# The first transform unit of a mixing one stretch later, and a mixing that ends with its last unit

## The chip, the cores and the metric

The kernel runs on one core of one Trainium2 chip. The metric is the device time of one execution in microseconds (us), as the median of several runs. A profile of one further execution shows every instruction of every engine: TensorE (PE) does the matrix products and the transposes, VectorE (DVE), ScalarE (ACT) and GpSimd (POOL) the elementwise work, SyncE (SP) issues most of the transfers.

## The reference

Two blocks in a row, all in fp32, for 8 batches, 8 heads, 576 positions and 64 values per head:

```python
scores = matmul(q, k.T) / sqrt(64)                    # (8, 8, 576, 576)
thresh = max(scores, -1) - tau
scores = where(scores >= thresh, scores, -1e9)
attn = exp(scores - max(scores)); attn /= sum(attn) + 1e-9
x = matmul(attn, v)                                   # rearranged to (8, 576, 512)

mixed = real(fft(fft(x, axis=1), axis=2))             # over positions, then over values
u = x + mixed
un = (u - mean(u)) / sqrt(var(u) + 1e-6)
out = u + maximum(un @ w_ch1, 0) @ w_ch2              # w_ch1 512x2048, w_ch2 2048x512
```

## The kernel before

The attention is cut into steps: a step is 128 queries (64 for the last) of a pair of heads, five steps make a pair of heads, four pairs a batch, so 20 steps make a batch (`per_batch`) and the eight batches 160 steps. A step computes the scores (`sc`, lines 440 and 446), takes their maximum (`neg`, VectorE, line 520), the exponentials (ScalarE, line 526), the threshold and the sum (VectorE, line 540), the division (ScalarE, line 549), and transposes the weights on TensorE (`pe`, line 587, and `pw`, line 605), which ScalarE copies out of PSUM. Twice in five steps the product with the values (`pv`, line 636) is made.

The two Fourier transforms of a batch are matrix products with cosine and sine tables. When the last pair of heads of a batch is done, its rows are folded (sums and differences of mirrored positions, lines 687 to 703, on VectorE for the last pair), and a generator `mixing` (line 728) does the rest in units, each ended by a `yield`. Its first three units are folds on VectorE into the tile `f` (lines 718 to 749). Six units follow in which TensorE multiplies `f` with the tables over the values (`py`, line 759) and ScalarE copies the result to `y_e` or `y_o` (line 764). The last five multiply with the tables over the positions (`pa`, lines 776 and 780), and VectorE and GpSimd add `x` and store to `u_t` (lines 796 to 805).

The channel products of the reference are done for groups of 512 rows, by a product of two levels with fewer multiplications, in the generator `two_level`: 28 items of first-level products (`ph`, line 1203) and 49 items of second-level products (`po`, line 1390). An item of `po` is four to eight matmuls and counts 2048 columns; seven items share two PSUM banks (four and three), which VectorE, ScalarE or GpSimd drain or add up (lines 1184, 1402 to 1410, 1255, 1336). A group can only begin when the mixing of its batch is at its end (`mixed`).

The order of everything is written out by hand[...]. From batch 2 on (line 1724) a step is a row of three stretches, and each has one call of `fill`. `fill` adds `per_slot` columns to a budget and works off items of the groups until what is spent reaches the budget. `per_slot` is set when a batch's mixing is started (`start_batch`, line 1622, in the step whose number in its batch is 2): what is to do, less `keep`, over 60 stretches. `keep` is thus the work that is left over when the next mixing starts. A unit of a mixing counts against the budget with what it yields, MIX / 11 for each matrix unit and nothing for the folds.

Units are taken by `mix(1)`. In step 2 of a batch the mixing begins: one unit after the first `fill`, one in the second. In step 3 the third fold is taken before the first `fill`, and so is one unit between the first and the second `fill`, one in the second and one in the third. From step 4 on there is one unit in each stretch. These are the lines in the loop:

```python
        fill(True)
        ...softmax_second(i), measure(), what was held...
        if mixes:
            mix(1)
        ...
        weights = weights_in_parts(i - 1) if i <= total else iter(())
        next(weights, None)          # pe and the first pw
        ...
        fill()
        next(weights, None)          # the second pw
```

`fill(True)` takes no unit of a mixing; `fill()` takes one before its items. PSUM tiles named pd, pm, pn, pe, pw, pv, py, pa, ph and po come from one ring of four banks with the tag "mm".

After the last step the remaining items and the last mixing follow in a tail, and then groups 7 and 8 alone.

Of the kernel before, what the change touches and what calls it, by code (L numbers as in the profile page):

```python
# [18 lines left out]
def _reversed(ap):  # L19

    n = ap.shape[1]
    return bass.AP(
        tensor=ap.tensor,
        offset=ap.offset + n - 1,
        ap=[list(ap.ap[0]), [-1, n]],
    )
# [21 lines left out]
def kernel(  # L48
# [14 lines left out]
    DM = H * D  # L63
# [5 lines left out]
    NJ = HID // 128  # L69
# [7 lines left out]
    BT = 512  # L77
# [645 lines left out]
    MIX = 4 * (3 * 5 * 128 + 5 * 2 * KH)  # L723
# [4 lines left out]
    def mixing(b):  # L728
# [43 lines left out]
        def over_seq(y, odd, cols, m):  # L772
            pa = ps.tile([128, 512], FP32, tag="mm", bufs=4, name="pa")
            for parity, u, table, extra in ((0, 0, seq_even, seq_xe), (1, 2, seq_odd, seq_xo)):
                at = pa[0:m, parity:KH:2]
                nc.tensor.matmul(  # L776
                    at, y[:, u, cols], table[:, odd, :], start=True, stop=False,
                    skip_group_check=True,
                )
                nc.tensor.matmul(  # L780
                    at, y[:, 1, cols], extra[:, odd, :], start=False, stop=True,
                    skip_group_check=True,
                )
            return pa

        settle(b)
        for t in range(2):
            cols = slice(128 * t, 128 * t + 128)
            tmp = sb.tile([128, 3, KH], FP32, tag="tmp", bufs=1, name="tmp")
            low, high, sin = (tmp[:, c, :] for c in range(3))  # L790
            pb = over_seq(y_o, 1, cols, 128)
            nc.scalar.copy(sin, pb[:, 0:KH])
            yield MIX / 11
            pa = over_seq(y_e, 0, cols, 128)

            nc.vector.tensor_tensor(out=low, in0=pa[:, 0:KH], in1=sin, op=ALU.subtract)  # L796
            nc.vector.tensor_tensor(out=high, in0=pa[:, 0:KH], in1=sin, op=ALU.add)
            def add(c, rows, first, second, eng=None):
                if eng is None:
                    eng = nc.vector if b == B - 1 and c % 2 else nc.gpsimd  # L800
                eng.tensor_tensor(  # L801
                    out=u_t[rows, c, slot.start : slot.start + KH],
                    in0=x[c][rows, 0:KH], in1=first, op=ALU.add,
                )
                eng.tensor_tensor(
                    out=u_t[rows, c, slot.start + KH : slot.stop],
                    in0=x[c][rows, KH:S], in1=_reversed(second[:, 1:HALF]), op=ALU.add,
                )

            every = slice(0, 128)  # L810
            add(t, every, low, high, nc.vector if b == 0 and t == 1 else nc.gpsimd)
            add(3 - t, every, high, low)
            if t == 1:
                add(3, slice(0, 1), high[0:1, :], low[0:1, :])
            yield MIX / 11
            if t == 1:

                pa = over_seq(y_e, 0, slice(256, 257), 1)
                nc.scalar.copy(sin[0:1, :], pa[0:1, 0:KH])
                add(2, slice(0, 1), sin[0:1, :], sin[0:1, :])  # L820
                yield MIX / 11


    warm = const.tile([128, 1], FP32, name="warm")
# [2 lines left out]
    def measure():  # L827
        while measures:
            measures.pop(0)()
# [5 lines left out]
    def cost(g):  # L835

        return (4 * BT * (NJ * ND + NJ * DM // 128) if g == 0 else COLS1 + COLS2) + ND * BT
# [59 lines left out]
    def channels(rows):  # L897
        for j in range(NJ):
            ht = hs[:, BT * j : BT * (j + 1)]
            ph = ps.tile([128, 512], FP32, tag="mm", bufs=4, name="ph")  # L900
            for c in range(ND):
                nc.tensor.matmul(  # L902
                    ph[:, :], w1[c][:, 128 * j : 128 * (j + 1)], u_t[:, c, 0:BT],
                    start=(c == 0), stop=(c == ND - 1),
                )
            if j % 2 == 0:
                nc.scalar.activation(out=ht, in_=ph[:, :], func=ACT.Relu)
            else:
                nc.vector.tensor_relu(ht, ph[:, :])
            yield 4 * ND * BT  # L910
            if j % 3 == 2 and j // 3 < 4:
                rows.load(j // 3)
                yield ND * 128
            if j == 12:
                rows.factors()
        def both():
            yield from w1_forms()
            ensure(1)
            while not next(forms_w2):
                yield  # L920

        forms = both()
        for t in range(4):
            po = ps.tile([128, DM], FP32, tag="mm", bufs=4, name="po")
            for j in range(NJ):
                nc.tensor.matmul(  # L926
                    po[:, :], hs[:, BT * j + 128 * t : BT * j + 128 * (t + 1)], w2[j],
                    start=(j == 0), stop=(j == NJ - 1),
                )
                if j % 2 == 1 and j < NJ - 1:  # L930
                    next(forms, None)
                    yield 2 * 4 * DM
            rows.add(t, slice(0, DM), po[:, :])
            rows.store(t)
            background()
            yield 2 * 4 * DM
        for _ in forms:
            pass
# [531 lines left out]
    mixes = []  # L1470
    mixed = 0
    work = []
    spent = budget = per_slot = 0.0
    per_batch = NPAIR * NT
# [143 lines left out]
    def fold_more():  # L1618
        if folds and next(folds[0], True):
            folds.pop(0)  # L1620

    def start_batch(b):

        nonlocal groups, todo, per_slot, budget
        mixes.append(mixing(b))
        todo += MIX
        while groups < NG and BT * (groups + 1) <= (b + 1) * S:
            rows = Rows(groups)
            work.append((b, channels(rows) if groups == 0 else two_level(groups, rows), rows))
            todo += cost(groups)  # L1630
            groups += 1

        keep = 4 * BT * NJ * DM // 128 if b == 0 else 3 * 7 * 2048
        per_slot = (todo - spent - keep) / (3 * per_batch)
        budget = spent

    def mix(count):
        nonlocal spent, mixed
        for _ in range(count):
            done = next(mixes[0], None)  # L1640
            if done is None:
                mixes.pop(0)
                mixed += 1
                break
            spent += done

# [77 lines left out]
    for i in range(2 * per_batch, total):  # L1724


        n, t = divmod(i, NT)
        values = iter(())
        if i < total:
            scores(i)  # L1730
        if t == 3 and i < total:
            values = values_in_parts(n, 0)
        elif t == 1 and n > 0:
            while folds:
                fold_more()
            values = values_in_parts(n - 1, 1)
        next(values, None)
        if i % per_batch == 3:
            next(values, None)
        if i < total:  # L1740
            softmax_first(i)
        next(values, None)
        if i % per_batch == 3:
            mix(1)
        if i % per_batch == 2:
            for _ in last_fold:
                pass
            start_batch(i // per_batch - 1)
        fill(True)
        if i < total:  # L1750
            softmax_second(i)
        measure()
        while held:
            held.pop(0)()
        if mixes:
            mix(1)
        if t == 1:
            if n % NPAIR:
                folds.append(fold_rows(n - 1))
            else:  # L1760
                last_fold = fold_rows(n - 1)
                next(last_fold)
        weights = weights_in_parts(i - 1) if i <= total else iter(())
        next(weights, None)
        if t > 2:
            fold_more()
        fill()
        if i % per_batch == 1:
            next(last_fold)
        next(weights, None)  # L1770
        if i < total:
            softmax_third(i)
            if t == 1:
                prep_ends(n)
            if t == 2 and n + 1 < B * NPAIR:
                scale_q(n + 1)
            if t == 3 and n + 1 < B * NPAIR:
                prep_pair(n + 1)
        if wanted:
            wanted.pop().factors()  # L1780
        if i % per_batch == 1:
            next(last_fold)
        fill(apart=i % per_batch == 2)
        if t == 2 and n + 1 < B * NPAIR:
            load_v(n + 1)
        if t == 4 and n + 2 < B * NPAIR:
            load_pair(n + 2)
# [89 lines left out]
```

## Time and profile before

| | |
|---|---|
| median of 3 runs | 1574.24 us (1571.42 to 1574.62) |
| the profiled execution | 1571.58 us, its span 1569.8 us, mean granted TensorE clock 0.996 |
| TensorE busy with matmuls | 1526.0 us |
| VectorE, ScalarE, GpSimd busy | 1061.6, 916.4, 777.5 us |
| DMA | 239.31 MB, 152 GB/s on average |

In the lines of the profile, L759 is line 759 of the kernel, `py<-dim_c,f` says that `py` is written from `dim_c` and `f`, and x4 that four instructions are merged. In the timeline the first number is the start in us from the span's start, the second the duration; what stands in brackets is the idle time of the engine ahead of the instruction and what ended it. In the waits the numbers are the sum in us, how often, and the longest.

### The profile page before, as it was taken

The page shows a single profiled execution, that of the slowest core. Times are in us where ns is not written, and L with a number is a line of the kernel's source. Part 1 is how long each engine was busy: PE and PEld are TensorE (multiplying, and loading weights), DVE is VectorE, ACT ScalarE, POOL GpSimd, SP SyncE. Part 2 cuts the span into 40 slices and gives each one's busy share as a digit, 9 for nine tenths or more (in the row PEclk, how much of TensorE's full clock was granted, in tenths as well). Part 3 has the DMA queues.
Part 4 walks back from the last instruction along what each step waited for, and adds up shares of the span by engine and source line. Part 5 has one row for each costly group of instructions (what it writes and reads, how often), then busy time and mean ns, then how long its engine had stood idle before and what let it go on. Part 6 is the DMA issues. An engine that isn't in the chain of part 4 may idle for free.

```text
span 1569.8 us, 27001 instructions
## 1 busy us (share of the span) xinstructions
PE 1526.0 (97%) x9786; PEld 1187.1 (76%) x9786; DVE 1061.6 (68%) x2119; ACT 916.4 (58%) x1921; POOL 777.5 (50%) x962
## 2 busy tenths in 40 slices
PE   8988989999999999999999999999999999999999
PEld 4555545556788778877787778877787878889999
DVE  7987776846869566776577566866577666745546
ACT  6875666554666666656766566657666666232231
POOL 3774553034455652546254724555264625546735
PEclk9999999999999999999999999999999999999999
DMA  6423231646956264634454345635464434646655
GB/s 166 130 58 117 77 90 24 204 147 180 323 154 214 73 188 122 185 111 144 144 173 149 116 135 153 184 103 158 130 185 137 141 118 149 222 141 235 235 201 182
DMA packets 248907, 239.31 MB, mean 152 GB/s; under 512 B 197027, under 2 KB 218533, under 8 KB 228678
## 3 DMA queue, kind: packets, MB, share of 16 engines
q1 hardware_dynamic: 246262, 237.28, 49.6%
q8 instruction: 78, 1.28, 0.3%
q10 hardware_dynamic: 2512, 0.30, 0.1%
q14 instruction: 55, 0.45, 0.1%
HBM read 205.93 MB, written 31.46 MB: 151 GB/s over the span
## 4 chain that ended last, share of the span: by engine, by line
PE 83%; DVE 9%; ACT 4%; issue 1%; DMA 1%; POOL 1%; SPq 0%; ACTq 0%; DVEq 0%
PE ph L1203 24%; PE po L1390 18%; PE pv L636 9%; PE sc L440 9%; PE pw L605 7%; PE po L926 4%; PE ph L902 3%; PE sc L446 2%; PE py L759 2%; PE pa L776 1%; PE pe L587 1%; DVE neg L461 1%; PE pn L851 1%; PE pa L780 1%; PE pd L111 1%
## 5 line engine op out<-in xcount | busy, mean ns | idle before, releaser
L520 DVE TENSOR_REDUCE neg<-sc 128x1 f32<-128x576 f32 x216 | 154.3, 751 | 131.4 <-PE sc L440 118.6
L526 ACT ACTIVATE e<-sc,neg 128x576 f32<-128x576 f32 x216 | 158.5, 734 | 120.7 <-DVE neg L520 120.7
L1390 PE MATMUL po<-w,w_all 128*128 128x128 f32 x1728 | 219.0, 277 | 0.3 <-ACT ends L593 0.3
L1140 DVE TENSOR_TENSOR hs<-ph,hs 128x512 f32<-128x512 f32 (+1 forms) x128 | 105.4, 823 | 161.1 <-PE ph L1203 104.0
L1390 PEld LDWEIGHTS po<-w,w_all 128*128 128x128 f32 x1728 | 204.9, 192 | 9.2 <-issue 6.2
L1149 POOL TENSOR_TENSOR w<-hs 128x512 f32<-128x512 f32 x32 | 42.1, 1320 | 317.8 <-ACT hs L1145 243.9
L540 DVE SCALAR_TENSOR_TENSOR e<-sc,thr,e 128x576 f32<-128x576 f32 x216 | 168.4, 813 | 19.9 <-ACT thr L530 19.6
L1203 PE MATMUL ph<-u_t,w 128*128 128x256 f32 x768 | 180.5, 382 | 0.6 <-DMA w<-f 0.4
L607 ACT COPY e_t<-pw 128x512 f32<-128x512 f32 x256 | 148.7, 595 | 45.8 <-PE pw L605 44.7
L605 PE MATMUL pw<-ident,e 128*128 128x128 f32 x1152 | 169.9, 275 | 5.6 <-ACT ends L593 2.2
L440 PE MATMUL sc<-kT,qT 64*128 64x288 f32 x1024 | 168.1, 431 | 6.6 <-DVE e L477 4.4
L549 ACT ACTIVATE e<-e,den 128x576 f32<-128x576 f32 x216 | 157.5, 775 | 8.5 <-DVE den L388 7.7
L1203 PEld LDWEIGHTS ph<-u_t,w 128*128 128x128 f32 x768 | 141.4, 190 | 23.2 <-issue 4.4
L1203 PE MATMUL ph<-w_all,w 128*128 128x256 f32 x672 | 157.1, 383 | 1.1 <-DVE w_all L1125 1.0
L605 PEld LDWEIGHTS pw<-ident,e 128*128 128x128 f32 x1152 | 135.4, 141 | 21.9 <-issue 5.6
L1203 PEld LDWEIGHTS ph<-w_all,w 128*128 128x128 f32 x672 | 123.6, 190 | 23.7 <-issue 4.9
L1145 ACT ACTIVATE hs<-hs 128x512 f32<-128x512 f32 (+1 forms) x96 | 74.1, 771 | 113.5 <-DVE hs L1140 112.8
L440 PEld LDWEIGHTS sc<-kT,qT 64*128 64x128 f32 x1024 | 95.7, 187 | 57.9 <-issue 26.8
L1255 POOL TENSOR_TENSOR w_all<-w_all 128x128 f32<-128x128 f32 (+2 forms) x160 | 116.9, 747 | 30.3 <-DVE w_all L1410 22.4
L1390 PE MATMUL po<-w,hs 128*128 128x128 f32 x912 | 119.4, 278 | 0.3 <-ACT ends L593 0.3
L1390 PEld LDWEIGHTS po<-w,hs 128*128 128x128 f32 x912 | 109.7, 192 | 9.7 <-issue 7.1
L801 POOL TENSOR_TENSOR u_t<-x,tmp 128x289 f32<-128x289 f32 (+1 forms) x45 | 33.9, 753 | 123.7 <-DVE tmp L796 123.7
(224 smaller groups left out, 2946.7 us busy)
## 6 DMA issues: line engine op xcount, KB each, us to landing
w<-f SPq DMA_DIRECT2D x150, 1024.0 KB, 4.9
hs<-in_moe_w_ch_dram SPq DMA_DIRECT2D x23, 512.0 KB, 5.2
q_in<-in_q_dram SPq DMA_DIRECT2D x128, 72.0 KB, 4.1
out_dram<-u SPq DMA_DIRECT2D x36, 256.0 KB, 2.3
k_in<-in_k_dram SPq DMA_DIRECT2D x124, 72.0 KB, 2.6
v_in<-in_v_dram SPq DMA_DIRECT2D x64, 128.0 KB, 5.0
f<-w SPq DMA_DIRECT2D x14, 512.0 KB, 3.9
f<-w SPq DMA_DIRECT2D x7, 1024.0 KB, 4.8
```

Source lines behind the costliest of these rows:

```text
L440: nc.tensor.matmul(sc[j][:, c, 0:HALF], qT[hp, 128 * t : 128 * t + 128], kT[hp, k0 + HALF * c : k0 + HALF * (c + 1)], start=True, stop=True,)
L520: nc.vector.tensor_reduce(out=neg[:, j : j + 1], in_=sc[j][:, :, 0:HALF], axis=AXIS_XY, op=ALU.max, negate=True,)
L526: nc.scalar.activation(out=ej, in_=sc[j][:, :, 0:HALF], func=ACT.Exp, bias=neg[:, j : j + 1], scale=1.0)
L540: nc.vector.scalar_tensor_tensor(out=ej, in0=sc[j][:, :, 0:HALF], scalar=thr[:, j : j + 1], in1=ej, op0=ALU.is_ge, op1=ALU.mult, accum_out ...
L549: nc.scalar.activation(out=e[:, S * j : S * (j + 1)], in_=e[:, S * j : S * (j + 1)], func=ACT.Copy, scale=den[:, j : j + 1],)
L605: nc.tensor.transpose(pw[:, c, :], e[:, c0 : c0 + 128], ident[:, :])
L607: nc.scalar.copy(e_t[:, 4 * j : 4 * j + 4, qs], pw[:, :, :])
L636: nc.tensor.matmul(pv[64 * j : 64 * j + 64, 0:m], vt[:, 2 * c + j, :], e_t[:, 4 * j + c, 0:m] if c < 4 else ends[:, 0, 0:m], start=(c == 0 ...
L1140: nc.vector.tensor_tensor(out=to, in0=bank, in1=to if other is None else other, op=ALU.add)
L1203: nc.tensor.matmul(bank[:, 256 * q : 256 * q + 256].rearrange("p (two n) -> p two n", two=2), left[:, 256 * c + 128 * q : 256 * c + 128 * ...
L1255: return lambda: eng.tensor_tensor(out=to, in0=to, in1=other, op=ALU.add)
L1390: nc.tensor.matmul(to, lefts[m][j][:, s], right_[:, 128 * s : 128 * (s + 1)], start=jn in (0, 4) and s == 0, stop=s == 3, skip_group_check ...
```

## The change

In step 3 of a batch no unit is taken between the first and the second `fill`, so the first unit with matmuls is taken in the second `fill`, and each later unit comes one stretch later than it did. The last `yield` of a mixing is taken away: the mixing ends in the same call that emits its last unit, and that unit's share is added to `spent` there. The work left over at the start of the next mixing is 23 items of 2048 columns instead of 21, for all batches but the first.

```diff
--- before
+++ after
@@ -818,7 +818,6 @@
                 pa = over_seq(y_e, 0, slice(256, 257), 1)
                 nc.scalar.copy(sin[0:1, :], pa[0:1, 0:KH])
                 add(2, slice(0, 1), sin[0:1, :], sin[0:1, :])
-                yield MIX / 11
@@ -1630,7 +1629,7 @@
-        keep = 4 * BT * NJ * DM // 128 if b == 0 else 3 * 7 * 2048
+        keep = 4 * BT * NJ * DM // 128 if b == 0 else 23 * 2048
         per_slot = (todo - spent - keep) / (3 * per_batch)
         budget = spent
@@ -1641,6 +1640,7 @@
             if done is None:
                 mixes.pop(0)
                 mixed += 1
+                spent += MIX / 11
                 break
             spent += done
@@ -1752,7 +1752,7 @@
         measure()
         while held:
             held.pop(0)()
-        if mixes:
+        if mixes and i % per_batch != 3:
             mix(1)
         if t == 1:
             if n % NPAIR:
```

## The prediction

> **What bounds the kernel now.** I read the page first, then TensorE's waits, then the timeline around those waits. The page gives the bound:
>
> ```profile
> PE 1526.0 (97%) x9786; PEld 1187.1 (76%) x9786; DVE 1061.6 (68%) x2119; ACT 916.4 (58%) x1921; POOL 777.5 (50%) x962
> ```
>
> TensorE (PE) is busy 97% of the span and no other engine is over 68%. The change removes no matmul, so it can only touch TensorE's idle time. The gaps over 0.1 us in its timeline add up to 38.9 us, 24.0 us of them ahead of 315 us, in code that is not touched. From the waits of TensorE (engine, what waited, released by what: total us, times, longest us):
>
> ```profile
> PE py L759 <- DVE f L740: 8.8, 5, 2.0
> ...
> PE py L759 <- DVE w_all L1410: 1.6, 1, 1.6
> PE py L759 <- ACT y_e L769: 0.7, 4, 0.2
> ...
> PE pw L605 <- DVE w_all L1410: 0.7, 1, 0.7
> ```
>
> The first row is the largest wait left. It is the first transform unit of a mixing (py, line 759) waiting for VectorE's last fold of the same mixing (line 740). The timeline puts its five instances at 507, 677, 850, 1023 and 1194 us (1.17, 1.51, 2.03, 2.02, 2.03 us). The mixing near 310 us, interleaved with longer matmuls, has none of them. One instance on TensorE:
>
> ```profile
> 1018.31 2.05 PE L1390 MATMUL po<-w,hs 128*128 128x128 f32 x16
> 1020.20 0.56 PE L759 MATMUL py<-dim_c,f 128*128 128x65 f32 x4
> 1022.78 0.49 PE L759 MATMUL py<-dim_c,f 128*128 128x128 f32 x2 [2.02 <-DVE f L740]
> 1023.10 0.27 PE L587 MATMUL pe<-ident,e 128*128 128x128 f32 x1
> 1023.21 0.60 PE L605 MATMUL pw<-ident,e 128*128 128x128 f32 x4
> 1024.01 0.71 PE L759 MATMUL py<-dim_s,f 128*128 128x128 f32 x4 [0.19 <-ACT y_e L769]
> ```
>
> and VectorE and GpSimd (POOL) beside it:
>
> ```profile
> 1019.63 0.55 DVE L1410 TENSOR_TENSOR w_all<-w_all,po 128x384 f32<-128x384 f32 x1
> 1020.09 1.42 DVE L520 TENSOR_REDUCE neg<-sc 128x1 f32<-128x576 f32 x2
> 1021.42 1.75 DVE L740 SCALAR_TENSOR_TENSOR f<-f,factors 128x304 f32<-128x304 f32 x2
> 1023.09 0.47 DVE L749 TENSOR_TENSOR f<-sums 128x304 f32<-128x304 f32 x1
> ```
>
> VectorE shows no idle from 1003.4 to 1026 us: it has a backlog, and the fold comes when that is worked off. Behind the waiting py stand transposes pe and pw (lines 587, 605) that need no fold: they started at once when py was through.
>
> [...] the ready transposes stood 2.02 us behind py. [...] the two folds took 1.75 us with GpSimd's line 1336 beside them (1020.32 to 1022.39 us) and 0.97 us at 676.41 us without it.
>
> **The change part by part.** (Lines from 822 to 1642 are one lower in the changed kernel.)
>
> 1. Step 3 of the late mixings. Its order on TensorE was sc, pv, two products po, py, pe, pw, py, pw, py, po. It becomes sc, pv, two po, pe, pw, py, po, pw, py, po. The transposes that came after py now come ahead of it: from 1023.10 to 1023.82 us, 0.72 us of work, so py reaches its third matmul 0.72 us later. For the last three instances: 1020.76 (end of its first two matmuls, when it stood waiting) plus 0.72 is about 1021.5 us.
>
> When is the fold ready? Call T the end of the first L740, about 1022.7 us now. The order on VectorE moves too, since the larger keep and the mixing's later units leave the products two items further back in this step. Between VectorE's last idle time and the fold there are now two more adds of line 1184 (0.6 us each from start to start) and one more pair of bn_stats and bn_aggr (0.79), and one drain of 384 columns (0.46) goes behind the fold: +1.5 us. Against that, the idle 1.03 us ahead of the first bn_stats goes, as its transposed rows come a stretch earlier, and GpSimd's line 1336, which follows that drain, can no longer lie on the fold: -0.75 us. Sum -0.3; I put T at 1022.6 us, give or take 1 us[...].
>
> After py comes a new item: po (0.9 us), then pw, whose PSUM bank is freed by the drain of 384 columns, now queued behind the folds: T + 0.85 (to the end of L749) + 0.5 + 0.1 = T + 1.45. Without any stall this pw would start at 1021.5 + 0.35 + 0.9 = 1022.75. So the stall left is T - 1021.3 = 1.3 us (0.3 to 2.3) against 2.2 now (2.02 and 0.19). Gain 0.9 each, three times: **2.7 us**.
>
> The instance at 507 us: stall 1.17 + 0.18 now, py needed at 505.8 + 0.7 = 506.5, T about 506.9 (two more adds less a drain, +0.75, and line 1336 off the fold, -0.77): 0.4 left. Gain **0.9**. At 677 us: 1.51 + 0.70 now. Two more adds and a bn pair less one row add are +1.6, idle times of 1.03 and 0.36 us go, T moves by +0.2, the shift is 0.72 and the drain no longer frees pw's bank: 0.95 left. Gain **1.25**.
>
> 2. Steps 4 to 6. Every unit moves by one stretch; the number of units in a stretch stays one. New is that in step 5 the first pa (line 776) follows the last py after only pe and pw, 0.72 us. It needs ScalarE's copy of that py (0.62 us, line 764), behind two exps of 0.74 us, which now end 3.65 us after the step's first sc begins; the copy is ready at about 4.35. The third matmul of pa, the first to read it, comes at 4.7 where two products precede py, and at 3.85 at 677's mixing, where one does. Cost nothing, and 0.5 us once. ScalarE's old wait of 2.29 us for GpSimd's adds (1043.17 us) goes, but TensorE did not wait there. The next group's first ph (line 1203) stands 7.1 us behind the last full pa instead of 5.3, so the adds into u_t stay covered.
>
> 3. The removed yield and the added spent. Together they leave the count equal; the mixing ends in the same third stretch of step 6. In the first two batches the sequence of matmuls is the same. Cost nothing.
>
> 4. keep from 43,008 to 47,104 columns: two items of 2048, 2 x 0.9 us of TensorE work, are left for later steps each time, none is added. The weight loads (w<-f on SP's queue) are issued by the items and move with them; they land in 4.8 us and TensorE waited 0.4 us for one in the whole run. In the tail, py now comes two items earlier but VectorE's fold stands ahead of two adds that delayed it (2.46 and 0.68 us). The 1.56 us stall at 1362.9 us becomes 0 to 1.5; I take **0.8** gained.
>
> 5. Everywhere else the products stand differently against the attention steps. Now such places cost single waits of 0.2 to 0.95 us, 3.3 us in all after 315 us apart from those above. A trace of before can't say which return: I take 0.5 us worse, bounds 3 better and 4 worse.
>
> Sum: 2.7 + 0.9 + 1.25 + 0.8 - 0.5 - 0.5 = 4.65 us. The profiled execution took 1571.58 us (span 1569.8 and 1.8 around it), which gives 1566.9. The median of the three runs is 2.7 us higher and the lowest is 1571.42, so by the median it is 1569.6; I name **1569.0 us**.
>
> **Rivals.** *All stalls go.* If GpSimd leaves VectorE alone for 1.3 us more, T is below 1021.3 and step 3 gives its whole 10.0 us (8.8, three of 0.19, 0.7), the tail 1.56: 11.5 us, 1562.7 by the median. For it speaks that three of five instances are alike to 0.01 us, so that what helps one helps all; against it the backlog.
>
> *VectorE later, slower than before.* If T comes over 0.8 us later than now (1023.5 us), pw behind the drain pays more than py saved. At 1024.6 us, [...] the stall is 3.3: 1.1 us lost three times, 0.85 at 507, 0.15 at 677, 0.5 at pa and 1 elsewhere, 5.8 us together: 1580 us by the median, 1577 by the profile. For it: two more adds in the window, and pw's new wait. Against it: the 1.03 us idle shows that part of the backlog is a late input.
>
> *It only moves.* T about 0.5 us later than now, the tail unchanged: within 1 us of 1574.
>
> **How the numbers follow.** A measurement of this kernel can tell about 0.2%, 3.1 us. Partial gain 0.5, all stalls gone 0.15, only moved 0.2, slower 0.15. Of the partial case about a fifth lies within 3.1 us. Faster 0.55, same 0.29, slower 0.16. The range runs from 1562.5 (all gone) to 1577 (the slower case by the profiled execution).
>
> **What would show it.** Right: py behind L740 falls from 8.8 to 2 to 5 us, with a new row pw behind L1410 of 0 to 3 us; L740 pairs near 0.97 us; no row of pa behind line 764 over 1 us. Wrong: py behind L740 at 8 us or more, a pw row over 4 us, or new waits in steps far from a mixing that add up to over 5 us.

## The result, and the profile after

| | before | after |
|---|---|---|
| median (lowest to highest), us | 1572.83 (1570.08 to 1577.07) | 1586.07 (1585.36 to 1589.2) |
| ratio to before, 95% interval | | 1.0085 (1.0071 to 1.0098) |
| span of the profiled execution | 1569.8 | 1587.4 |

The change made the kernel slower by 0.85%, 13.2 us. The forecast was 1569.0 us with a range of 1562.5 to 1577: wrong in sign, and the time lies outside the range. The page of the changed kernel, first part:

```profile
PE 1532.6 (97%) x9786; PEld 1188.9 (75%) x9786; DVE 1073.9 (68%) x2119; ACT 914.8 (58%) x1921; POOL 786.7 (50%) x962
```

TensorE has the same 9786 matmuls and bounds the kernel as it did. What it waits for has changed. TensorE's waits in the changed kernel (what waited, released by what: total us, times, longest us; lines from 822 to 1642 are one lower than before):

```profile
PE py L759 <- DVE f L740: 6.5, 5, 1.5
...
PE po L1389 <- DVE w_all L1183: 4.0, 2, 3.0
PE py L759 <- DVE w_all L1409: 3.3, 3, 1.1
PE ph L1202 <- DVE hs L1139: 3.2, 10, 0.4
...
PE pw L605 <- ACT x L643: 1.4, 1, 1.4
PE py L759 <- ACT y_e L769: 1.3, 1, 1.3
PE pa L776 <- ACT y_o L764: 1.3, 3, 0.9
```

The row that the change aims at fell from 8.8 to 6.5 us. Six rows under it are new or have grown: in before, no product waited as long as 0.15 us for the add (line 1184 there), ph behind line 1140 had one wait of 0.3 us, pw behind `x` one of 0.4.

The loss can be split. I add up TensorE's idle times over 0.15 us, the shortest that the timeline shows, take the time lost where the windows view shows a granted clock under 1.0, and call what is left of the span "rest":

| profiled execution | span | waits over 0.15 us | lost to the clock | rest |
|---|---|---|---|---|
| before | 1569.8 | 38.9 | 6.8 | 1524.1 |
| after | 1587.4 | 50.3 | 10.2 | 1526.8 |
| after less before | 17.6 | 11.4 | 3.4 | 2.7 |

The difference is larger than the 13.2 us of the medians, since the profiled execution of the changed kernel is the slowest of its six. The 2.7 us are in no listed wait: TensorE's matmuls are themselves recorded as busy for 6.6 us longer (1526.0 us in before), more than the 3.4 us of the clock; why was not followed up.

In this section and the next, a step is a step of the attention, and the late mixings are the five of batches 2 to 6. The 11.4 us of waits by place: step 3 of the five late mixings -2.0 (10.0 to 8.0); steps 4 and 5 +6.4 (0 to 6.4); first-level products behind line 1140 in the middle +2.5 (0.31 to 2.8); 384 to 462 us +2.4 (0.4 to 2.8); the tail +1.45; ahead of 315 us +0.6, though TensorE's order first differs at 307 us. The gain is there. It is smaller than forecast, and more than given back in places where nothing, or much less, waited before. One late mixing on TensorE in the changed kernel (its timeline; the time in brackets is the idle time before the instruction):

```profile
1028.53 0.56 PE L759 MATMUL py<-dim_c,f 128*128 128x65 f32 x4
1030.17 0.49 PE L759 MATMUL py<-dim_c,f 128*128 128x128 f32 x2 [1.08 <-DVE f L740]
1030.87 1.16 PE L1389 MATMUL po<-w,hs 128*128 128x128 f32 x8 [0.21 <-ACT ends L593]
...
1036.49 0.65 PE L759 MATMUL py<-dim_c,f 128*48 128x65 f32 x6
...
1038.94 0.64 PE L759 MATMUL py<-dim_s,f 128*48 128x128 f32 x4 [1.11 <-DVE w_all L1409]
1039.87 0.66 PE L605 MATMUL pw<-ident,e 128*128 128x128 f32 x4 [0.28 <-ACT y_e L769]
```

The same stretch on VectorE, with GpSimd's add beside it:

```profile
1035.81 1.26 POOL L1183 TENSOR_TENSOR w_all<-hs 128x512 f32<-128x512 f32 x1 [2.17 <-PE po L1389]
1035.88 1.75 DVE L1183 TENSOR_TENSOR w_all<-w_all,hs 128x512 f32<-128x512 f32 x1
1037.55 0.74 DVE L520 TENSOR_REDUCE neg<-sc 128x1 f32<-128x576 f32 x1
1038.22 0.67 DVE L1409 TENSOR_TENSOR w_all<-w_all,po 128x512 f32<-128x512 f32 x1
```

The wait for the fold is 1.08 instead of 2.02 us. But the unit of 48 rows, now in step 4, stands 1.11 us behind a drain: it starts 0.05 us after line 1409 ends at 1038.89. Ahead of that drain stand, without a gap, an add of line 1183 and the maximum of the step's scores. The add takes 1.75 us, with GpSimd's add of the same line running from 1035.81 to 1037.07 us; the one in the tail below takes 0.68.

The tail, TensorE and then VectorE:

```profile
1375.58 1.16 PE L1389 MATMUL po<-w,w_all 128*128 128x128 f32 x8 [3.02 <-DVE w_all L1183]
```

```profile
1370.68 2.79 DVE L740 SCALAR_TENSOR_TENSOR f<-f,factors 128x304 f32<-128x304 f32 x2
1373.39 1.53 DVE L749 TENSOR_TENSOR f<-sums 128x304 f32<-128x304 f32 x1
1374.84 0.68 DVE L1183 TENSOR_TENSOR w_all<-hs 128x512 f32<-128x512 f32 x1
```

The fold did come ahead of the adds, as the prediction has it. But now a product waits for such an add: 3.02 us, where 1.56 us was lost in the tail before.

### The profile page after: what moved, and what is told of

It is laid out like the page before. It is cut to its first block, busy times and chain, and to the rows that moved or that the text cites. A ratio compares the mean times of both kernels' runs of the same rounds, so it can differ in the third digit from the quotient of the medians.

```text
span 1587.4 us, 27017 instructions
## 1 busy us (share of the span) xinstructions
PE 1532.6 (97%) x9786; PEld 1188.9 (75%) x9786; DVE 1073.9 (68%) x2119; ACT 914.8 (58%) x1921; POOL 786.7 (50%) x962
## 4 chain that ended last, share of the span: by engine, by line
PE 80%; DVE 11%; ACT 5%; issue 2%; DMA 1%; POOL 1%; DVEq 0%; SPq 0%; ACTq 0%
PE ph L1202 24%; PE po L1389 17%; PE pv L636 9%; PE sc L440 9%; PE pw L605 6%; PE po L925 4%; PE ph L901 3%; PE sc L446 2%; PE pa L776 1%; PE pa L780 1%; DVE neg L461 1%; PE pe L587 1%; PE py L759 1%; DVE e L540 1%; DVE w_all L1183 1%
```

## The experiments

Theory A: the time is lost to `keep`. With 23 items the channel products stand two items further back against every step, and TensorE meets other waits; the shift alone costs little or nothing. Against it stands that the shift itself loses, because its units meet other buffers in step 4. The first four kernels take the change apart.

**e1, keep alone.** Before, with:

```diff
-        keep = 4 * BT * NJ * DM // 128 if b == 0 else 3 * 7 * 2048
+        keep = 4 * BT * NJ * DM // 128 if b == 0 else 23 * 2048
```

> The kernel before with one edit: keep is 23 items instead of 21; the mixing begins and ends as before. Theory A (the two items left over move the drains and adds of the products against the attention steps, and that makes the new waits): the loss is here, 1582 to 1588 us, the wait of 3.0 us for the add of line 1184 in the tail and the 0.31 us waits of ph for line 1140 come back, and py behind line 740 stays near 8.8 us. Theory B (the units of the mixing, one stretch later, make the waits themselves): within 3 us of before, 1570 to 1576 us, none of these waits. Theory C (each edit makes a part): 1576 to 1581 us.

Measured: 1587.06 us (1586.45 to 1589.82), before 1572.69, ratio 1.0095 (1.0073 to 1.0117). The whole loss of the change, without the shift. The profiled execution is 16.0 us longer than that of before: 7.7 us in waits, 5.1 lost to the clock and 3.2 in the rest. Its waits on TensorE:

```profile
PE py L759 <- DVE f L740: 12.0, 5, 2.9
...
PE po L1390 <- DVE w_all L1184: 4.0, 2, 3.0
PE ph L1203 <- DVE hs L1140: 3.2, 10, 0.4
...
PE pw L605 <- ACT x L643: 1.4, 1, 1.4
```

Three of the grown rows of the changed kernel are here to the digit: the product behind the add, ph and pw behind `x`. They come with keep. The fold's row is 3.2 us worse than in before, so in the changed kernel the shift first had to win that back.

**e2, the shift with 21 items.** After, with keep undone:

```diff
-        keep = 4 * BT * NJ * DM // 128 if b == 0 else 23 * 2048
+        keep = 4 * BT * NJ * DM // 128 if b == 0 else 3 * 7 * 2048
```

> The changed kernel with keep back at 21 items; the first transform unit is still in the second stretch and the mixing still ends with its last unit. Theory A: the new waits go and part of the saving is seen, 1568 to 1573 us; py behind line 740 falls below 5 us; the wait of 1.11 us of py in step 4 behind the drain of line 1410 goes. Theory B: 1583 to 1587 us, that wait stays at 1.1 us in four mixings. Theory C: 1576 to 1581 us.

Measured: 1572.34 us (1568.78 to 1575.07), ratio 0.9994 (0.9984 to 1.0004). The shift is worth nothing. Its waits:

```profile
PE py L759 <- DVE f L740: 5.1, 4, 1.5
PE py L759 <- ACT y_e L769: 4.8, 4, 1.2
PE py L759 <- ACT ends L593: 2.0, 1, 2.0
PE pa L776 <- ACT y_o L764: 2.0, 7, 0.9
```

The fold's row falls from 8.8 to 5.1 (with 2.0 at 677 us now put down to a ScalarE copy), and 4.8 us appear in step 4 and about 1.6 of the pa row in step 5, behind copies that stand after the exps on ScalarE. So the shift does bring waits of its own in step 4, but they only cancel the gain.

**e3, the ending alone.** Before, with the last `yield` taken away and `spent += MIX / 11` added:

> The kernel before with one edit: the last yield is taken out and its share added to spent when the mixing ends. All theories: the order on TensorE is nearly that of before, within 3 us of it, 1570 to 1576 us.

Measured: 1572.92 us (1570.86 to 1578.12), ratio 1.0004 (0.9994 to 1.0014). Nothing, as the prediction had it.

**e4, the shift with 19 items.** After, with `19 * 2048`:

> The changed kernel with keep of 19 items, so that the products stand two items further on than with 21 and four further than with 23. Theory A: the time goes with the place of the products, not with the shift: another value than with 21 or 23, most likely 1572 to 1582 us. Theory B: 1583 to 1588 us, as with 23, since the units stand where they stand there.

Measured: 1584.65 us (1582.12 to 1586.9), ratio 1.0076 (1.0056 to 1.0095). Fewer items left cost nearly as much as more of them. The time lies in the range of theory B, but e2 has the same shift and loses nothing. So neither the shift nor the number put off costs as such, and 21 is a good place for this order.

**e7 and e8, where keep costs.** Before, with 23 items for a part of the batches only:

```diff
 e7:  keep = ... else (23 if b >= 6 else 21) * 2048
 e8:  keep = ... else (23 if b < 6 else 21) * 2048
```

> The kernel before with 23 kept items only for the last setting of the budget (the mixings of batch 6 and after), 21 for the others. Theory A (each place pays for itself): e1 lost 6.6 us from the first scores of step 142 to the end, where 1.8 us are the two items that were put off, and about 2 us in each of the five stretches between mixings before. So the last setting alone gives 1572.7 + 5 to 7 = 1578.7 (1577 to 1580.5), with the wait of 3.0 us of a product for line 1184 in the tail. Rival (the loss lies in the middle alone and the end only collects it): 1572 to 1574. Rival (the end alone): 1586 to 1588.

> The complement: 23 kept items for the mixings of batches 1 to 5, 21 for the last setting. Theory A: 1587.06 less the 5 to 7 us of the end, 1581 (1579 to 1583), with waits behind line 740 of 1.6 to 2.9 us in the middle and the end as in before. Rival (end alone): 1572 to 1574.

Measured: e7 1573.58 us, ratio 0.9997 (0.9985 to 1.0009); e8 1585.53 us, ratio 1.0081 (1.0066 to 1.0096). My expectation for e7 was wrong: the last setting alone costs nothing, and its tail has no wait of 3.0 us. For e8 I expected 1579 to 1583 us. The loss comes with the settings of batches 1 to 5; which of them carry it was not tried. e8 has the 0.31 us waits of ph (3.3 us in all), and 10.9 us behind line 740.

**e5 and e6, TensorE's clock.** In e1's trace each of the five waits for the fold is followed by a stretch at half clock. In the windows view of e1 (start and end; length; busy us of PE, PEld, DVE, ACT, POOL with counts; then the granted clock, DMA share and GB/s):

```profile
853.04:856.45 3.41, 0.68 (x6) 0.68 (x7) 3.41 (x7) 1.71 (x4) 0.62 (x1) 1.00 0.00 0
856.45:859.86 3.41, 3.39 (x18) 2.53 (x16) 3.31 (x10) 2.49 (x7) 2.09 (x1) 0.50 0.00 0
```

In the first 3.41 us TensorE is busy for 0.68, in the next its clock is 0.50: half of 3.41, 1.7 us, is counted as lost on top of the wait. To keep TensorE busy in the wait, six matmuls without use were added ahead of the third matmul of the first unit's py, for batches 2 to 6. They write columns 384 to 512 of `py`, which no copy reads (the expectation below has it that the next matmul overwrites them; it writes columns 129 to 257):

```diff
                 for c, c0, c1 in SIN if odd else COS:
+                    for _ in range(6 if c == 2 and u == 0 and 1 < b < B - 1 else 0):
+                        nc.tensor.matmul(
+                            py[:, 384:512], ones[:, :], ones[:, :],
+                            start=True, stop=True, skip_group_check=True,
+                        )
```

e5 is e1 with this, e6 is before with this.

> The kernel before with 23 kept items (as in e1, 1587.06 us) and six added matmuls of 128x128 (ones times ones, into columns of py that the next matmul overwrites) ahead of the third matmul of the first py of each of the mixings of batches 2 to 6. TensorE executes them while it would stand waiting for the fold of line 740. Theory C (TensorE's clock): in e1 each of the five waits of 1.6 to 2.9 us is followed by about 3.4 us at a granted clock of 0.50, which costs 1.7 us each time. If it is the idle stretch that brings the low clock, it goes when the stretch is shorter: the waits behind line 740 shrink by about 1.3 us each and end at the same times, no stretch at 0.50 follows them, and the time falls by 5 x 1.7 = 8.5 us to 1578.5 (1577 to 1581). Rival (the low clock has another cause, or costs nothing): the fold comes when it came, the low clock stays, 1587 (1586 to 1589).

> The same six added matmuls in the kernel before with its own 21 items. Theory C: before has the low clock after one to three of its five waits, and not in the same places in each execution, so the gain is 1.5 to 4 us: 1570 (1568.5 to 1571.5). Rival: 1572.7 to 1573.5, since the shortest wait (1.17 us at 507 us) is a little shorter than six matmuls.

Measured: e5 1583.49 us (1580.49 to 1586.87), ratio 1.0066 (1.005 to 1.0081); e6 1570.24 us (1567.72 to 1573.14), ratio 0.9983 (0.9975 to 0.9991). In neither trace is the clock low after a wait of step 3, and the mean granted clock is 0.996 in e5 against 0.992 in e1, and 0.999 in e6 against 0.996 in before; e1 had the low clock after all five waits. So it did not follow where TensorE was kept busy in the wait, and matmuls without use made the kernel 3.1 us faster than before. The size for e5 was too large: I reckoned 8.5 us from one trace, and the two ratios to before differ by 0.0029, 4.6 us. And e5 is still 13.25 us over e6, nearly the 14.4 us of e1 over before: the clock is real, but it is not the main part of what keep costs.

**e13, the same in the changed kernel.** After, with the six matmuls.

> The changed kernel with the six added matmuls of e6 ahead of the third matmul of the first py. Its waits there are 1.0 to 1.5 us and only one of them (858 us) was followed by a half clock in its profile, against the 1.3 us that six matmuls take. If the changed kernel loses its time to waits and not to the clock: 1585 (1583 to 1587), that is 14 us more than the kernel before with the same six matmuls (1570.24 in e6). If the clock is what keep costs: 1576 or less.

Measured: 1586.34 us (1582.64 to 1589.54), ratio 1.0083 (1.0065 to 1.0101). As expected if waits cost the time: unchanged, 16.1 us over e6. Its trace has no half clock after a wait of steps 3 to 5, and 44.4 us of waits against 32.8 in e6.

**e9 and e10, the shift without the rest.** Both are before with 21 items, and only step 3 is changed. e10 takes the first unit after the first pw, and the second unit directly behind it, so that all later units stay in place. e9 works off the second stretch's products ahead of the first unit:

```diff
 both:
-        if mixes:
+        if mixes and i % per_batch != 3:
             mix(1)
 e10, ahead of the second fill:
+        if i % per_batch == 3:
+            mix(1)
 e9, at the second fill, and again ahead of the third:
-        fill()
+        fill(apart=i % per_batch == 3)
+        if i % per_batch == 3:
+            mix(1)
...
+        if i % per_batch == 3:
+            mix(1)
```

> The kernel before with its 21 items; only step 3 is changed. Its second stretch works off its two products before the first py unit instead of after it, and the third stretch takes its first unit ahead of its fill, so that all units of step 3 stay in step 3 and step 4 is as in before. Order on TensorE: sc, pv, two po, pe, pw, two po, py, pw, py, py (48 rows). Theory D (the first unit is worth moving back as long as nothing else moves): the third matmul of py comes 0.72 + 1.8 us later than in before, at 1023.3 us in the count of the prediction, after the fold (1022.7), so the five waits behind line 740 (8.8 us) and the 1.3 us of py and pw after them go, and with them the stretches at half clock (3.1 us in e6): 1561 (1558 to 1566). Rival (what was waited for in step 3 is waited for in step 4, as in e2, where py of 48 rows and pa waited 1.2 and 0.2 to 0.9 us each): 1570 to 1573.

> The kernel before with its 21 items; only step 3 is changed: the first py unit comes after pe and the first pw (0.72 us later), as in the changed kernel, but the second unit follows it at once and all later units stay where they are in before. This is the part of the change that the prediction priced, without the shift of steps 4 to 6. If that price was right (0.9 us three times, 0.9, 1.25): 1568.5 (1566 to 1570.5). If the fold simply comes 0.7 us later as well: 1572 to 1574.

Measured: e10 1569.99 us (1567.47 to 1574.0), ratio 0.9977 (0.9968 to 0.9986), inside its range. e9 1583.63 us (1581.72 to 1585.34), ratio 1.0062 (1.0044 to 1.0079): 22.6 us over the 1561 that I expected, and neither theory had it. e9's timeline on TensorE and on VectorE:

```profile
1026.35 1.06 PE L1390 MATMUL po<-w,w_all 128*128 128x128 f32 x8
...
1030.35 0.68 PE L759 MATMUL py<-dim_s,f 128*128 128x128 f32 x4 [0.94 <-DVE f L749]
1033.91 1.09 PE L759 MATMUL py<-dim_c,f 128*48 128x65 f32 x6 [2.88 <-DVE w_all L1410]
```

```profile
1027.04 2.77 DVE L740 SCALAR_TENSOR_TENSOR f<-f,factors 128x304 f32<-128x304 f32 x2
...
1032.59 0.67 DVE L1184 TENSOR_TENSOR w_all<-w_all,hs 128x512 f32<-128x512 f32 x1
1033.17 0.68 DVE L1410 TENSOR_TENSOR w_all<-w_all,po 128x512 f32<-128x512 f32 x1
```

The 2.02 us wait for the fold is gone. In its place stands a wait of 2.88 us for the drain of a product that was issued ahead of the unit, since that drain is queued behind the fold on VectorE. Over the five late mixings the waits of step 3 add up to 17.6 us against 10.0, and six windows at half clock follow them, against one in before. What was put ahead of the wait needed the same late engine.

**e14, both small gains.** e10 with the six matmuls.

> e10 (1569.99 us: the first py unit after the first pw, all other units where they are in before, 21 items) with the same six matmuls. Its waits for the fold are 0.64, 1.49, 1.49, 1.49 us, with 2.04 at 679 us for ScalarE, which comes earlier in py and stays. The profile of e10 had half clock at 680 and 854 us. If the two gains are of different kinds and add: 1569.99 less one or two stretches of 1.7, plus 0.7 at 508 us where the six take longer than the wait: 1568 (1566.5 to 1569.5). If e10's gain was already the clock: 1570 to 1571.

Measured: 1569.6 us (1566.96 to 1574.07), ratio 0.998 (0.9973 to 0.9987). Not told from e6 or e10: the gains do not add. e10's waits in step 3 are only 1.1 us shorter than before's in sum (8.9 against 10.0). That the rest of its gain is the clock fits e14 but was not shown: the one trace of e10 has half clock after two of the five waits at its first unit, that of before after one.

**e11, e12 and e15, other amounts kept.** Before, with `28 * 2048`, `30 * 2048` and `22 * 2048`.

> The kernel before with 28 kept items instead of 21. Theory E (what counts is where the mixing stands in the products' cycle of seven items, four and three to a pair of PSUM banks, since it decides which adds and drains VectorE has ahead of the fold and where first-level products wait): 28 leaves the same place in the cycle as 21, so 1574 (1571 to 1578), waits behind line 740 near 8.8 us. Rival (each item put off costs, 7 us each in the changed kernel): 1600 or more.

> The same with 30 items, two off the cycle as 23 is. Theory E: 1587 (1583 to 1590), about 13 us over e11, with waits behind line 740 of 10 to 12 us and the row of ph behind line 1140 near 3 us. Rival (each item costs): 1610 or more. Rival (the cycle does not matter): the same as e11.

> The kernel before with 22 kept items, one more than before and one fewer than the changed kernel. If each item that the products fall behind brings its own waits: about half of e1's 14.4 us, 1580 (1577 to 1583). If it is a matter of which add stands ahead of which wait, it can lie anywhere between 1572 and 1590, and the rows tell which: waits behind line 740 above 8.8 us, ph behind line 1140 above 0.9, a product behind line 1184 in the tail.

Measured: 28 items 1605.92 us, ratio 1.021 (1.0187 to 1.0234); 30 items 1581.65 us, ratio 1.0055 (1.0036 to 1.0075); 22 items 1581.59 us, ratio 1.0055 (1.0037 to 1.0072). Theory E, that the place in the cycle of seven decides, has fallen: 28, in the same place as 21, is the worst. Its first wait:

```profile
PE ph L1203 <- DMA w<-f: 10.7, 5, 2.2
```

Each amount brings rows of its own: here weights that land 2.0 to 2.2 us late in every late batch. Half clock takes 21.1 us in this profile, 14.3 more than in before's, so waits are only about half of its loss. With 22 items the ph row is 0.31 us twice a batch again, and pw waits 0.70 us behind line 1410 at three late mixings, not one. It lies where a cost for each item would put it, but 28 and 30 do not. From 21 to 30 items the time goes 1573, 1582, 1587, 1606, 1582: no slope, but an order with or without unlucky neighbours.

One thing sets the orders apart in the traces. VectorE's 108 adds of line 1184 take 97.1 us in before and 96.8 in e2, both with 21 items, but 106.6 in e1 and 111.0 in the changed kernel. In these four traces no add takes over 0.70 us unless GpSimd is at work beside it; over 0.8 us are 28 in before and in e2, 45 in e1 and 53 in the changed kernel. So with 23 items GpSimd's work falls on VectorE's adds more often (in the changed kernel 73 of the 108 have some of it beside them, in before 51), and VectorE is the engine that TensorE waits for in the three largest of the grown rows. How much of the loss this carries was not tested, and it does not order the kernels: with 28 items, the slowest, the adds take 102.5 us. Why 21 is a good amount stays open.

## Why the prediction was wrong

In this section a part is one of the five numbered parts of the prediction.

*Part 4, keep.* This is the step of the prediction that failed. It counted the two items, found that "none is added", and gave the end a gain of 0.8 us. e1 shows 14.4 us lost. The items cost nothing by themselves (e7); what costs is that the products stand two items back against the attention under the settings of batches 1 to 5 (e8). I followed that only in two places, the fold (part 1) and the tail. What it does there is only in part accounted for: of the 16.0 us in e1's profile 7.7 are waits, and e5 and e6 leave 13.25 us of loss where no low clock follows a wait for the fold.

*Part 5, the rest.* That cost belonged here, at "0.5 us worse, bounds 3 better and 4 worse". The trace has 4.9 us far from a mixing (ph behind line 1140 +2.5, 384 to 462 us +2.4), just under the 5 us that the prediction named as a sign of being wrong, and 2.7 us in no listed wait. The bounds came from the waits that before shows. They bound what can go, not what can come: a wait that the present order just avoids is in no row of it.

*Part 2, steps 4 to 6 of the attention.* "The number of units in a stretch stays one. Cost nothing, and 0.5 us once." The pa wait came in the one mixing that was named, at 0.88 us (700 us) for the 0.5 priced. The unit of 48 rows, and the pw behind it, were overlooked: the unit stands in a step 4 where the drain or copy that frees its bank is behind the maximum or the exp. This is 5.5 us here and, behind `y_e`, 4.8 us in e2, where with the pa row it used up the whole gain of the shift.

*Part 1, step 3 of the attention.* Right in mechanism, too large in size: py behind line 740 fell to 6.5 us, not to 2 to 5. For the three late instances 1.3 us was to be left; 1.54, 1.08 and 1.54 are, and with the new pw and po waits beside them 1.96, 1.29 and 2.18. At 507 us 0.4 was to be left and 1.50 is; at 677 us 0.95, and 1.05 is. In sum 2.0 us gained, not 4.85. The folds did run at 0.96 us for the pair at 1029.60 us, as I had it without GpSimd beside them.

*The tail.* The term of 0.8 us gained was 1.45 us lost: the fold, at 2.79 and 1.53 us, moved ahead of an add that a product needs.

*Part 3* was right: e3 is within 0.1% of before.

*The rivals.* "VectorE later, slower than before" has the right sign and the wrong place: it wanted T over 0.8 us later, and py's wait became shorter. The loss was bigger than its 5.8 us because it sat in places for which it allowed 0.5 and 1 us.

*Not in the prediction:* the clock. The changed kernel's trace has six stretches of 3.41 us at half clock, that of before four; counted at 1.7 us each, they make 3.4 of the 17.6 us between the two profiled executions; by e13, whose six matmuls leave the changed kernel's median where it was, the medians owe them next to nothing.

*Two readings* were off, without weight in the sum: the 38.9 us of gaps are those over 0.15 us (over 0.1 us there are 40.0), and the change begins to act at 307 us, not 315.

## What to carry to other kernels

When a hand-written order is nearly full (here 97%), that moving work costs nothing can only be said when the waits of the new order are worked out everywhere that it shifts. A list of the present waits bounds the gain, not the loss, so a phase shift through the whole kernel deserves a wide range on the slow side. A unit moved away from a late producer should not be put behind a buffer which that same engine has to drain (in e9 2.88 us for the 2.02 that went); and an edit of several parts is best priced, and tried, part by part: e10, the one part that was the point, is 0.23% faster, and the amount that came with it cost four times that.

## What the runs showed of the hardware

TensorE's half-clock stretches lie on a grid in these traces. In before they begin at 11.34, 83.02, 199.08 and 851.02 us, in the changed kernel at 83.09, 103.57, 199.15, 281.07, 857.92 and 1376.74 us, and each lasts 3.41 us. The distances from one to the next are 21, 34 and 191 times 3.413 us in before, and 6, 28, 24, 169 and 152 times in the changed kernel, to 0.02 of it. In e1 the last three begin at 856.45, 1030.53 and 1204.61 us, twice 51 times 3.413 us apart. A stretch of this grid, a window below, was not idle throughout where half clock followed it. Before, in the windows view cut on its grid:

```profile
847.59:851.00 3.41, 1.38 (x13) 1.23 (x11) 3.41 (x6) 1.84 (x4) 2.07 (x1) 1.00 0.91 305
851.00:854.41 3.41, 3.30 (x17) 2.34 (x14) 3.34 (x9) 2.49 (x7) 0.00 (x0) 0.50 0.21 80
...
1018.26:1021.67 3.41, 2.50 (x22) 2.31 (x20) 3.41 (x8) 1.10 (x3) 1.35 (x1) 1.00 0.37 72
1021.67:1025.08 3.41, 2.11 (x15) 1.71 (x15) 3.41 (x7) 2.41 (x8) 0.72 (x1) 1.00 0.76 312
1025.08:1028.49 3.41, 3.41 (x27) 3.02 (x27) 3.30 (x9) 2.69 (x6) 1.28 (x1) 1.00 0.03 7
```

The wait of 2.03 us at 850 us lies within one window, which is busy for 1.38 of 3.41 us, and the next runs at 0.50. The wait of 2.02 us at 1023 us falls across a border, into windows busy for 2.50 and 2.11 us, and no low clock follows. In the traces of before and of the changed kernel together, windows at full clock in which TensorE was busy for 0.43 to 1.45 us were followed by half clock 8 times of 8, from 1.61 to 2.39 us 2 times of 26, from 2.40 us on never in 877; in e1 one busy for 1.52 us was followed by it. So of two waits of 2 us in before, one was followed by a stretch that is counted as 1.7 us lost and the other by none; that it turns on where the grid lies in an execution is my reading of them. The same wait was not followed alike in each execution: e3, whose waits for the fold are those of before to 0.02 us, has half clock after four of the five (mean granted clock 0.991), before after one (0.996). Where the same wait stands in each of five mixings, a few cheap matmuls in it (e6) were worth 3.1 us.
